# Batch 0's front in another order: zero products, V's spread and the release of the weights

## The chip, the cores and the metric

One core of one Trainium2 chip runs the kernel. The metric is the device time of one execution in microseconds (us); the time before is the median of three runs. Engines: PE (TensorE) multiplies, DVE (VectorE), ACT (ScalarE) and POOL (GpSimd) do the elementwise work, SP (SyncE) issues transfers. PE writes only into PSUM, and DVE or ACT copies from there.

## The reference

Eight batches of linear attention (8 heads, 576 positions, 64 features a head) and behind it a mixer with low rank along the positions and a two-layer network along the channels:

```python
def phi(x, c, s):                      # c, s: cos and sin of pi/2 * position / 576
    r = np.maximum(x, 0.0)
    return np.concatenate([r * c, r * s], axis=-1)
q_p, k_p = phi(q, cos_w, sin_w), phi(k, cos_w, sin_w)
kv  = np.einsum('bhsf,bhsd->bhfd', k_p, v)
num = np.einsum('bhsf,bhfd->bhsd', q_p, kv)
den = np.einsum('bhsf,bhf->bhs', q_p, k_p.sum(axis=2))[..., None] + 1e-06
x   = (num / den).transpose(0, 2, 1, 3).reshape(8, 576, 512)
u   = x + (x.transpose(0, 2, 1) @ U @ V).transpose(0, 2, 1)     # U 576x32, V 32x576
out = u + np.maximum(u @ w_ch1, 0.0) @ w_ch2                    # 512x2048, 2048x512
```

## The kernel before

**Tiling.** The 576 positions of a batch are four chunks of 128 (`c` = 0 to 3) and a tail of 64 (`c` = 4); the tails of two batches share one tile (`q_tl`, `k_tl`, `v_tl`, `x_tl`). q, k and v come in float32 into one staging tile each (`qst`, `kst`, `vst`), which every batch uses again; `load_odd` and `load_even` (L74, L68) fill a batch's odd and even partitions from SP's queue.

**Batch 0's front.** While q is on its way, PE multiplies zeros (`keep_warm`, L193). Then, chunk by chunk, `q_prep` makes the features (cos and sin, L258 on ACT, L260 on DVE; `FEATS` says which engine takes which), `qtr_mm` transposes them on PE (L328) and `qtr_evac` copies the transposes out. The same features for k follow, with `z_ps`, the sum of k's features over all positions (L807). `first_chain` then does all of batch 0 up to the mixer: casts of v (`v_block`, `v_prep`), `kv_unit` for heads 0 to 3 and 4 to 7 (L299), denominators (`den_mm`, L677; `recip`, L363 and L364), the products q times kv of half the heads for one chunk (`xh_mm`, L688) and their division (`xh_norm`, L697). `a_mm` (L715, L723) multiplies U by half the columns of x. `open_mm` (L730) puts the transposed x into PSUM, and `uTd_mm` (L488) adds the low-rank term to it, so that `uTd_evac` copies out u transposed, one of four blocks `d`. `spread_v` (L223, L226) brings V from 32 rows into the layout that `uTd_mm` and `u_unit` read (`V_bf`, `V_tl`).

**Mixer.** From `g1_main` (L523; hidden layer) and `g2_part` (L576; output) on, an order written out by hand puts the attention of the later batches beside the mixer's products: `at(j, ...)` for batch 1, `PLAN` for the rest. Batch 1's v is cast at slot 15, its kv products stand at slots 16 and 17.

**Queues and weights.** Each engine works in program order. POOL issues the loads of the weights, `w1_load` (L96) and `w2_load` (L102), four pieces each. Ahead of each group a copy of one element into `mark` makes POOL wait: in the kernel before for batch 0's v and for batch 1's v (heads 0 to 3).

**PSUM.** Tiles take buffers by tag: `X` one of two banks, `T` one bank, `o` two, `g` three (`O2`, `G3`, `T1` in the code). A new tile of a tag waits for the last reader of the one whose buffer it takes. `ORD`, the order of chunks behind kv, is (4, 0, 1, 2, 3).

Of the kernel before, what the change touches and what calls it, by code (L numbers as in the profile page):

```python
# [10 lines left out]
FP32 = mybir.dt.float32  # L11
# [6 lines left out]
def kernel(  # L18
# [15 lines left out]
    S = 576  # L34
    D = 64
    E = D + 1
    P = 128
# [5 lines left out]
    TS = 64  # L43
# [11 lines left out]
    ps = ctx.enter_context(tc.tile_pool(name="ps", bufs=1, space=bass.MemoryType.PSUM))  # L55
# [5 lines left out]
    kst = const.tile([P, H, 5, D], FP32)  # L61
# [44 lines left out]
    def cast(eng, o, i):  # L106
        if eng is nc.scalar:
            nc.scalar.activation(out=o, in_=i, func=AF.Copy, bias=0.0, scale=1.0)
        else:
            eng.tensor_copy(out=o, in_=i)  # L110
# [79 lines left out]
    def keep_warm(n, tag, bufs):  # L190
        w_ps = ps.tile([P, 512], FP32, tag=tag, bufs=bufs, name="w_ps")
        for _ in range(n):
            nc.tensor.matmul(out=w_ps, lhsT=zero[:, 0:P], rhs=zero, start=True, stop=True)  # L193
# [24 lines left out]
        for i in range(2):  # L218
            cast(G_, U_bf[tail(i), 4 + i, :], stU[tail(i), 4, :])

    def spread_v(eng):
        v_ps = ps.tile([P, 2, 512], FP32, tag="X", bufs=1, name="v_ps")
        nc.tensor.matmul(  # L223
            out=v_ps[:, 0, :], lhsT=four, rhs=V_nat[:, 0:512], start=True, stop=True
        )
        nc.tensor.matmul(  # L226
            out=v_ps[:, 1, 0:TS], lhsT=four, rhs=V_nat[:, 512:S], start=True, stop=True
        )
        cast(eng, V_bf, v_ps[:, 0, :].rearrange("r (c p) -> r c p", c=4))
        cast(eng, V_tl, v_ps[:, 1, 0:TS])  # L230


    k_p, q_p, q_pT, kv_sb, x_bf = {}, {}, {}, {}, {}
# [57 lines left out]
    def kv_unit(b, hg, tag, bufs, eng=None, n=E):  # L291
        if b not in kv_sb:
            kv_sb[b] = pool.tile([P, H, E], BF16, tag="kv", bufs=2, name="kv")
        acc = ps.tile([P, 4, n], FP32, tag=tag, bufs=bufs, name="kv_ps")
        vx = v_ext[b % 2]
        for i in range(4):
            h = hg * 4 + i
            for c in range(5):
                nc.tensor.matmul(  # L299
                    out=acc[:, i, :],  # L300
                    lhsT=k_of(b, c, h),
                    rhs=v_tl[:, h, 0:n] if c == 4 and b < 2 else vx[:, c, h, 0:n],
                    start=(c == 0),
                    stop=(c == 4),
                )
        cast(eng or V_, kv_sb[b][:, hg * 4 : hg * 4 + 4, 0:n], acc)
# [26 lines left out]
    def qtr_evac(b, c, eng, t):  # L333
        if c < 4:
            cast(eng, q_pT[b][:, c, :, :], t)
        else:
            cast(eng, q_tlT[:, :, tail(b)], t[:, :, 0:P:2])
# [24 lines left out]
    def recip(rec, den):  # L362
        nc.vector.tensor_scalar(out=rec, in0=den, scalar1=1e-6, scalar2=None, op0=ALU.add)  # L363
        nc.vector.reciprocal(out=rec, in_=rec)  # L364
# [42 lines left out]
    def A_of(b):  # L407
        return A_sb[b % 4]
# [57 lines left out]
    uT_ps = {}  # L466
# [16 lines left out]
    def uTd_evac(b, d, eng):  # L483
        cast(eng, uT[b][:, :, d, :], uT_ps[b, d])

    def uTd_mm(b, d):
        t = uT_ps[b, d]
        nc.tensor.matmul(  # L488
            out=t.rearrange("m c t -> m (c t)"), lhsT=A_of(b)[:, d * P : d * P + P],
            rhs=V_bf.rearrange("r c t -> r (c t)"), start=False, stop=True,  # L490
        )
# [182 lines left out]
    def den_mm(b, h0, h1, d_ps):  # L674
        for c in range(5):
            for h in range(h0, h1):
                nc.tensor.matmul(  # L677
                    out=d_ps[:, c, h - h0 : h - h0 + 1],
                    lhsT=qT_of(b, c, h),
                    rhs=z_sb[:, h : h + 1],  # L680
                    start=True,
                    stop=True,
                )

    def xh_mm(b, c, h0, tag, bufs):
        acc = ps.tile([P, 4, D], FP32, tag=tag, bufs=bufs, name="xh_ps")
        for h in range(h0, h0 + 4):
            nc.tensor.matmul(  # L688
                out=acc[:, h - h0, :], lhsT=qT_of(b, c, h), rhs=kv_sb[b][:, h, 0:D],
                start=True, stop=True,  # L690
            )
        return acc

    def xh_norm(b, c, h0, rec, acc):
        x_alloc(b)
        rows = slice(0, P) if c < 4 else tail(b)
        nc.vector.tensor_tensor(  # L697
            out=x_of(b, c, rows)[:, h0 * D : h0 * D + 4 * D].rearrange(
                "p (i d) -> p i d", d=D
            ),  # L700
            in0=acc[rows],
            in1=rec[rows, c, :].unsqueeze(2).to_broadcast([P if c < 4 else TS, 4, D]),
            op=ALU.mult,
        )
# [23 lines left out]
    def open_mm(b, d, t, cs):  # L728
        for c in cs:
            nc.tensor.matmul(  # L730
                out=t[:, c, :], lhsT=x_bf[b][:, c, d * P : d * P + P], rhs=ident,
                start=(c == 0), stop=False,
            )

    def first_chain(b):
        v_block(b, 0, 4, 0, 3, V_)
        v_block(b, 0, 4, 3, 4, A_)
        v_prep(b, 0, 4, (4,), (A_,))
        cast(V_, z_sb, z_ps)
        v_block(b, 4, 8, 0, 3, V_)  # L740
        v_block(b, 4, 8, 3, 4, A_)
        v_prep(b, 4, 8, (4,), (A_,))
        d0 = ps.tile([P, 2, 512], FP32, tag="X", bufs=1, name="d_ps")
        d = [d0[:, 0, 0:20].rearrange("p (c h) -> p c h", h=4)]
        rec = [pool.tile([P, 5, 4], FP32, tag="rec5", bufs=2, name="rec5") for _ in (0, 1)]
        kv_unit(b, 0, *T1, None, D)
        den_mm(b, 0, 4, d[0])
        recip(rec[0], d[0])
        x0 = [xh_mm(b, c, 0, *G3) for c in ORD[0:3]]
        for n in (0, 1):  # L750
            xh_norm(b, ORD[n], 0, rec[0], x0[n])
        kv_unit(b, 1, *O2, A_, D)
        x0.append(xh_mm(b, ORD[3], 0, *O2))
        d1 = ps.tile([P, 512], FP32, tag="T", bufs=1, name="d_ps")
        d.append(d1[:, 0:20].rearrange("p (c h) -> p c h", h=4))
        den_mm(b, 4, 8, d[1])
        x0.append(xh_mm(b, ORD[4], 0, *O2))
        for n in range(2, 5):
            xh_norm(b, ORD[n], 0, rec[0], x0[n])
            if n == 3:  # L760
                recip(rec[1], d[1])
        x1 = [xh_mm(b, c, 4, *t) for c, t in zip(ORD, (T1, G3))]
        spread_v(A_)
        x1 += [xh_mm(b, c, 4, *t) for c, t in zip(ORD[2:], (G3, G3, O2))]
        for n in range(5):
            xh_norm(b, ORD[n], 4, rec[1], x1[n])
        uT_alloc(b)
        u03 = ps.tile([P, 2, 512], FP32, tag="X", bufs=1, name="u03")
        t = [u03[:, i, :].rearrange("p (c t) -> p c t", c=4) for i in range(2)]
        a_ps = ps.tile([P, DM], FP32, tag="o", bufs=2, name="a_ps")  # L770
        a_mm(b, a_ps, 0, 256, range(5))
        cast(A_, A_of(b)[:, 0:256], a_ps[:, 0:256])
        for tag, bufs in (T1, O2):
            t.insert(-1, ps.tile([P, 4, P], FP32, tag=tag, bufs=bufs, name="uT_ps"))
        for i in range(4):
            uT_ps[b, i] = t[i]
        for i in range(2):
            open_mm(b, i, t[i], range(4))
        uTd_mm(b, 0)
        uTd_evac(b, 0, A_)  # L780
        uTd_mm(b, 1)
        uTd_evac(b, 1, V_)
        a_mm(b, a_ps, 256, 512, range(5))
        cast(A_, A_of(b)[:, 256:512], a_ps[:, 256:512])
        open_mm(b, 3, t[3], range(4))
        open_mm(b, 2, t[2], range(4))

    FEATS = [(V_, V_ if c == 3 else A_) for c in TL]
    qT_alloc(0)
    keep_warm(13, "X", 1)  # L790
    t_q = []
    for c in TL:
        tg = G3 if c < 3 else O2
# [1 line left out]
    for c in TL:  # L795
        q_prep(0, c, FEATS[c])
        qtr_mm(0, c, 0, H, t_q[c])
        keep_warm(1, "X", 1)
    for c, eng in zip(TL, (V_, A_, V_, A_, V_)):
        qtr_evac(0, c, eng, t_q[c])  # L800
    keep_warm(4, "X", 1)
    z_all = ps.tile([P, 2, 512], FP32, tag="X", bufs=1, name="z_ps")
    z_ps = z_all[:, 0, 0:H]
    for c in TL:
        k_prep(0, c, FEATS[c])
        for h in range(H):
            nc.tensor.matmul(  # L807
                out=z_ps[:, h : h + 1], lhsT=k_of(0, c, h), rhs=v_tl[:, 0, D:E],
                start=(c == 0 and h == 0), stop=(c == 4 and h == H - 1),
            )  # L810
        keep_warm(1, *G3)

    cast_uv()
    G_.tensor_copy(out=mark, in_=vst[0:TS, 3, 4, 0:1])
    for n in range(4):
        w1_load(n)
    first_chain(0)
    load_odd(qst, q, 1)
    load_even(qst, q, 1)
    load_odd(kst, k, 1)  # L820
# [1 line left out]
    for h0 in (0, 4):  # L822
        load_odd(vst, v, 1, h0, h0 + 4)
        load_even(vst, v, 1, h0, h0 + 4)
    G_.tensor_copy(out=mark, in_=vst[0:TS, 3, 4, 0:1])
    for n in range(4):
        w2_load(n)
    g1_main(0, 0, True)
# [109 lines left out]
```

## Time and profile before

| | |
|---|---|
| time, median of 3 (lowest, highest) | 313.95 us (313.73, 314.32) |
| the profiled execution: its time, its span | 311.89 us, 310.1 us |
| busy in the span: PE, DVE, ACT, POOL | 97%, 50%, 44%, 17% |
| granted TensorE clock | 1.0 |
| read from HBM, written | 36.86 MB, 9.44 MB |
| first product of the mixer (L523) | 22.46 us |

A line of a timeline gives start, duration, engine, line, operation, out<-in, shape and count, and in brackets the idle time before it and who ended it. A line of the chain gives start, duration, engine, tile, line. PE's products are pipelined and their ends modelled, so starts tell more than ends; the granted clock is given in tenths of full speed for 40 equal slices of the span.

### The profile page before, as it was taken

The page shows a single profiled execution, that of the slowest core. Times are in us where ns is not written, and L with a number is a line of the kernel's source. Part 1 is how long each engine was busy: PE and PEld are TensorE (multiplying, and loading weights), DVE is VectorE, ACT ScalarE, POOL GpSimd, SP SyncE. Part 2 cuts the span into 40 slices and gives each one's busy share as a digit, 9 for nine tenths or more (in the row PEclk, how much of TensorE's full clock was granted, in tenths as well). Part 3 has the DMA queues.
Part 4 walks back from the last instruction along what each step waited for, and adds up shares of the span by engine and source line. Part 5 has one row for each costly group of instructions (what it writes and reads, how often), then busy time and mean ns, then how long its engine had stood idle before and what let it go on. Part 6 is the DMA issues. An engine that isn't in the chain of part 4 may idle for free.

```text
span 310.1 us, 5750 instructions
## 1 busy us (share of the span) xinstructions
PE 301.9 (97%) x2341; PEld 157.7 (51%) x2341; DVE 155.0 (50%) x342; ACT 136.0 (44%) x229; POOL 52.9 (17%) x96
## 2 busy tenths in 40 slices
PE   5999999999999999999999999999999999999995
PEld 1676454446655444574455444574455444474443
DVE  4979834896878584146327583046426520002111
ACT  2936730264820466679300366669300366640000
POOL 8410400510131008004221300003321000000000
PEclk9999999999999999999999999999999999999999
DMA  7999999979997979982999879912981240001131
GB/s 216 354 258 255 197 187 274 326 143 241 288 191 142 314 133 251 243 242 82 180 212 322 207 127 234 273 47 53 194 154 60 75 80 0 0 2 68 70 101 68
DMA packets 86027, 53.21 MB, mean 172 GB/s; under 512 B 54258, under 2 KB 83218, under 8 KB 86002
## 3 DMA queue, kind: packets, MB, share of 16 engines
q1 hardware_dynamic: 79298, 41.36, 57.5%
q0 software_dynamic: 6560, 11.43, 15.0%
q8 instruction: 18, 0.29, 0.4%
q10 hardware_dynamic: 144, 0.07, 0.1%
q14 instruction: 7, 0.06, 0.0%
HBM read 36.86 MB, written 9.44 MB: 149 GB/s over the span
## 4 chain that ended last, share of the span: by engine, by line
PE 90%; DVE 5%; DMA 2%; issue 1%; ACT 0%; ACTq 0%; DVEq 0%
PE o_ps L576 40%; PE g_ps L523 32%; PE gt_ps L543 5%; PE kv_ps L299 3%; PE x_ps L390 3%; PE va_ps L435 2%; DMA qst<-in_q_dram 2%; DVE q_p L260 2%; DVE k_p L260 2%; PE a_ps L415 1%; PE t_ps L328 1%; PE t_ps L316 1%; PE w_ps L193 0%; PE va_ps L438 0%; PE xh_ps L688 0%
## 5 line engine op out<-in xcount | busy, mean ns | idle before, releaser
L532 ACT ACTIVATE hid<-g_ps 128x512 bf16<-128x512 f32 x128 | 76.2, 598 | 106.2 <-PE g_ps L523 106.2
L576 PE MATMUL o_ps<-w_bf,hid 128*128 128x512 bf16 (+2 forms) x528 | 120.0, 372 | 0.0
L523 PE MATMUL g_ps<-uT,w_bf 128*128 128x512 bf16 x512 | 117.6, 379 | 0.0
L523 PEld LDWEIGHTS <-w_bf 128*128 128x128 bf16 x512 | 48.9, 98 | 58.0 <-issue 2.1
L576 PEld LDWEIGHTS <-hid 128*128 128x128 bf16 x528 | 48.2, 98 | 50.8 <-issue 0.8
L586 DVE TENSOR_TENSOR o_sb<-u_bf,o_ps 128x512 f32<-128x512 bf16 (+2 forms) x33 | 22.1, 669 | 56.3 <-PE o_ps L576 56.2
L597 POOL DMA_DIRECT2D out_dram<-o_sb x24 | 15.2, 633 | 126.2 <-DVE o_sb L586 67.0
L442 DVE TENSOR_TENSOR u_bf<-x_bf,va_ps 128x512 bf16<-128x512 bf16 x32 | 21.8, 685 | 10.0 <-PE va_ps L435 9.9
L110 POOL CAST v_ext<-vst 128x512 bf16<-128x512 f32 (+1 forms) x28 | 20.1, 744 | 37.1 <-DMA vst<-in_v_dram 36.9
L110 DVE CAST kv<-kv_ps 128x260 bf16<-128x260 f32 (+1 forms) x15 | 6.4, 429 | 36.9 <-PE kv_ps L299 36.9
L400 DVE TENSOR_TENSOR x_bf<-x_ps,rec 128x512 bf16<-128x512 f32 x28 | 19.4, 691 | 1.0
L363 DVE TENSOR_SCALAR rec<-x_ps 128x8 f32<-128x8 f32 (+1 forms) x35 | 5.8, 165 | 22.8 <-PE x_ps L390 22.3
L543 PE MATMUL gt_ps<-uT_tl,w_bf 128*128 128x128 bf16 x256 | 15.9, 219 | 0.0
L260 DVE TENSOR_SCALAR q_p<-qst,cosw 128x512 bf16<-128x512 f32 x24 | 13.7, 583 | 2.9 <-DMA qst<-in_q_dram 2.9
L543 PEld LDWEIGHTS <-w_bf 128*128 128x128 bf16 x256 | 14.7, 98 | 0.9
L576 PE MATMUL o_ps<-w_bf,hid_tl 128*128 128x512 bf16 x64 | 14.8, 379 | 0.0
L390 PEld LDWEIGHTS <-q_pT 128*128 128x128 bf16 x224 | 10.7, 98 | 6.4 <-DVE x_bf L400 0.4
L258 ACT ACTIVATE k_p<-kst,sinw 128x512 bf16<-128x512 f32 x19 | 13.3, 712 | 0.0
L299 PEld LDWEIGHTS <-k_p 128*128 128x128 bf16 x256 | 11.1, 97 | 3.2 <-issue 0.3
L550 ACT ACTIVATE hid_tl<-gt_ps 128x512 bf16<-128x512 f32 x16 | 9.6, 597 | 6.6 <-PE gt_ps L543 6.6
L435 PE MATMUL va_ps<-A_sb,V_bf 128*128 128x512 bf16 x32 | 12.1, 379 | 0.1
L390 PE MATMUL x_ps<-kv,q_pT 128*128 128x65 bf16 x224 | 11.8, 194 | 0.0
(128 smaller groups left out, 233.0 us busy)
## 6 DMA issues: line engine op xcount, KB each, us to landing
qst<-in_q_dram SPq DMA_DIRECT2D x14, 512.0 KB, 6.3
kst<-in_k_dram SPq DMA_DIRECT2D x14, 512.0 KB, 8.6
vst<-in_v_dram SPq DMA_DIRECT2D x12, 512.0 KB, 8.1
out_dram<-o_sb POOLq DMA_DIRECT2D x24, 256.0 KB, 3.7
w_bf<-in_moe_w_ch_dram POOLq DMA_DIRECT2D x8, 512.0 KB, 11.1
out_dram<-o_sb SPq DMA_DIRECT2D x7, 256.0 KB, 2.4
qst<-in_q_dram SPq DMA_DIRECT2D x2, 640.0 KB, 6.4
kst<-in_k_dram SPq DMA_DIRECT2D x2, 640.0 KB, 10.8
```

The source lines that it names most:

```text
L110: eng.tensor_copy(out=o, in_=i)
L260: eng.tensor_scalar(out=o, in0=i, scalar1=0.0, scalar2=w, op0=ALU.max, op1=ALU.mult)
L299: nc.tensor.matmul(out=acc[:, i, :], lhsT=k_of(b, c, h), rhs=v_tl[:, h, 0:n] if c == 4 and b < 2 else vx[:, c, h, 0:n], start=(c == 0), st ...
L390: nc.tensor.matmul(out=acc[:, g, i * E : i * E + E], lhsT=qT_of(b, c, h), rhs=kv_sb[b][:, h, :], start=True, stop=True,)
L400: nc.vector.tensor_tensor(out=x_of(b, c, rows).rearrange("p (g i d) -> p g i d", g=2, d=D), in0=view[:, :, :, 0:D], in1=rec[rows].unsqueez ...
L435: nc.tensor.matmul(out=va, lhsT=V_bf[:, c, :], rhs=A_of(b), start=True, stop=True)
L442: nc.vector.tensor_tensor(out=u_bf[b][:, c, :] if c < 4 else u_tl[b // 2], in0=x_of(b, c), in1=va, op=ALU.add,)
L523: nc.tensor.matmul(out=g_ps.rearrange("p (c t) -> p c t", c=4), lhsT=w1_bf[:, d, j * P : j * P + P], rhs=uT[b][:, :, d, :], start=(d == 0) ...
L532: nc.scalar.activation(out=hid[b][:, j, :], in_=g_ps, func=AF.Relu, bias=0.0, scale=1.0)
L543: nc.tensor.matmul(out=g_ps[:, jj, :], lhsT=w1_bf[:, d, j * P : j * P + P], rhs=uT_tl[pr][:, d, :], start=(d == 0), stop=(d == 3),)
L576: nc.tensor.matmul(out=o[:, cols], lhsT=lhs[:, j, c * P : c * P + P], rhs=w2_bf[:, j, cols], start=(j == 0), stop=(j == NJ - 1),)
L586: nc.vector.tensor_tensor(out=o_sb[:, cols], in0=u[:, cols], in1=o[:, cols], op=ALU.add)
```

## The change

It has four parts. The zero products ahead of q go from 13 to 24, the single ones between q's transposes go, and the two features of one chunk on DVE are those of chunk 0 instead of chunk 3; chunk 0's transposes are copied out before chunk 2's features. V's spread moves from the middle of the second head group to the front: its products stand before `first_chain`, its copies on ACT behind the first `recip`. In `first_chain` the first kv goes out on ACT, the second kv product follows three `xh` products, all five divisions of the first head group come ahead of those of the second, `a_mm` and two `open_mm` come before the last second-group products, and copies change engines. The load of w_ch1 waits for batch 0's k, that of w_ch2 for batch 1's k.

```diff
--- before.py
+++ after.py
@@ -218,16 +218,19 @@
         for i in range(2):
             cast(G_, U_bf[tail(i), 4 + i, :], stU[tail(i), 4, :])
 
-    def spread_v(eng):
-        v_ps = ps.tile([P, 2, 512], FP32, tag="X", bufs=1, name="v_ps")
+    def spread_mm():
+        t = [ps.tile([P, 512], FP32, tag="o", bufs=2, name="v_ps") for _ in (0, 1)]
         nc.tensor.matmul(
-            out=v_ps[:, 0, :], lhsT=four, rhs=V_nat[:, 0:512], start=True, stop=True
+            out=t[0], lhsT=four, rhs=V_nat[:, 0:512], start=True, stop=True
         )
         nc.tensor.matmul(
-            out=v_ps[:, 1, 0:TS], lhsT=four, rhs=V_nat[:, 512:S], start=True, stop=True
-        )
-        cast(eng, V_bf, v_ps[:, 0, :].rearrange("r (c p) -> r c p", c=4))
-        cast(eng, V_tl, v_ps[:, 1, 0:TS])
+            out=t[1][:, 0:TS], lhsT=four, rhs=V_nat[:, 512:S], start=True, stop=True
+        )
+        return t
+
+    def spread_evac(eng, t):
+        cast(eng, V_bf, t[0].rearrange("r (c p) -> r c p", c=4))
+        cast(eng, V_tl, t[1][:, 0:TS])
 
 
     k_p, q_p, q_pT, kv_sb, x_bf = {}, {}, {}, {}, {}
@@ -732,7 +735,7 @@
                 start=(c == 0), stop=False,
             )
 
-    def first_chain(b):
+    def first_chain(b, v_ps):
         v_block(b, 0, 4, 0, 3, V_)
         v_block(b, 0, 4, 3, 4, A_)
         v_prep(b, 0, 4, (4,), (A_,))
@@ -740,54 +743,49 @@
         v_block(b, 4, 8, 0, 3, V_)
         v_block(b, 4, 8, 3, 4, A_)
         v_prep(b, 4, 8, (4,), (A_,))
-        d0 = ps.tile([P, 2, 512], FP32, tag="X", bufs=1, name="d_ps")
-        d = [d0[:, 0, 0:20].rearrange("p (c h) -> p c h", h=4)]
+        d_ps = ps.tile([P, 2, 512], FP32, tag="X", bufs=1, name="d_ps")
+        d = [d_ps[:, i, 0:20].rearrange("p (c h) -> p c h", h=4) for i in (0, 1)]
         rec = [pool.tile([P, 5, 4], FP32, tag="rec5", bufs=2, name="rec5") for _ in (0, 1)]
-        kv_unit(b, 0, *T1, None, D)
+        kv_unit(b, 0, *T1, A_, D)
         den_mm(b, 0, 4, d[0])
         recip(rec[0], d[0])
+        spread_evac(A_, v_ps)
         x0 = [xh_mm(b, c, 0, *G3) for c in ORD[0:3]]
-        for n in (0, 1):
+        kv_unit(b, 1, *T1, A_, D)
+        den_mm(b, 4, 8, d[1])
+        x0 += [xh_mm(b, c, 0, *O2) for c in ORD[3:5]]
+        for n in range(5):
             xh_norm(b, ORD[n], 0, rec[0], x0[n])
-        kv_unit(b, 1, *O2, A_, D)
-        x0.append(xh_mm(b, ORD[3], 0, *O2))
-        d1 = ps.tile([P, 512], FP32, tag="T", bufs=1, name="d_ps")
-        d.append(d1[:, 0:20].rearrange("p (c h) -> p c h", h=4))
-        den_mm(b, 4, 8, d[1])
-        x0.append(xh_mm(b, ORD[4], 0, *O2))
-        for n in range(2, 5):
-            xh_norm(b, ORD[n], 0, rec[0], x0[n])
-            if n == 3:
+            if n == 2:
                 recip(rec[1], d[1])
-        x1 = [xh_mm(b, c, 4, *t) for c, t in zip(ORD, (T1, G3))]
-        spread_v(A_)
-        x1 += [xh_mm(b, c, 4, *t) for c, t in zip(ORD[2:], (G3, G3, O2))]
-        for n in range(5):
-            xh_norm(b, ORD[n], 4, rec[1], x1[n])
+        x1 = [xh_mm(b, c, 4, *t) for c, t in zip(ORD, (T1, G3, G3, G3))]
+        xh_norm(b, ORD[0], 4, rec[1], x1[0])
         uT_alloc(b)
-        u03 = ps.tile([P, 2, 512], FP32, tag="X", bufs=1, name="u03")
-        t = [u03[:, i, :].rearrange("p (c t) -> p c t", c=4) for i in range(2)]
         a_ps = ps.tile([P, DM], FP32, tag="o", bufs=2, name="a_ps")
         a_mm(b, a_ps, 0, 256, range(5))
         cast(A_, A_of(b)[:, 0:256], a_ps[:, 0:256])
-        for tag, bufs in (T1, O2):
-            t.insert(-1, ps.tile([P, 4, P], FP32, tag=tag, bufs=bufs, name="uT_ps"))
-        for i in range(4):
-            uT_ps[b, i] = t[i]
+        u03 = ps.tile([P, 2, 512], FP32, tag="X", bufs=1, name="u03")
+        uT_ps[b, 0] = u03[:, 0, :].rearrange("p (c t) -> p c t", c=4)
+        uT_ps[b, 3] = u03[:, 1, :].rearrange("p (c t) -> p c t", c=4)
+        for i, (tag, bufs) in ((1, O2), (2, T1)):
+            uT_ps[b, i] = ps.tile([P, 4, P], FP32, tag=tag, bufs=bufs, name="uT_ps")
         for i in range(2):
-            open_mm(b, i, t[i], range(4))
-        uTd_mm(b, 0)
-        uTd_evac(b, 0, A_)
-        uTd_mm(b, 1)
-        uTd_evac(b, 1, V_)
+            open_mm(b, i, uT_ps[b, i], range(4))
+        xh_norm(b, ORD[1], 4, rec[1], x1[1])
+        x1.append(xh_mm(b, ORD[4], 4, *G3))
+        for n in range(2, 5):
+            xh_norm(b, ORD[n], 4, rec[1], x1[n])
+        for i in range(2):
+            uTd_mm(b, i)
+            uTd_evac(b, i, A_)
         a_mm(b, a_ps, 256, 512, range(5))
-        cast(A_, A_of(b)[:, 256:512], a_ps[:, 256:512])
-        open_mm(b, 3, t[3], range(4))
-        open_mm(b, 2, t[2], range(4))
-
-    FEATS = [(V_, V_ if c == 3 else A_) for c in TL]
+        cast(V_, A_of(b)[:, 256:512], a_ps[:, 256:512])
+        open_mm(b, 2, uT_ps[b, 2], range(4))
+        open_mm(b, 3, uT_ps[b, 3], range(4))
+
+    FEATS = [(V_, V_ if c == 0 else A_) for c in TL]
     qT_alloc(0)
-    keep_warm(13, "X", 1)
+    keep_warm(24, "X", 1)
     t_q = []
     for c in TL:
         tg = G3 if c < 3 else O2
@@ -795,10 +793,11 @@
     for c in TL:
         q_prep(0, c, FEATS[c])
         qtr_mm(0, c, 0, H, t_q[c])
-        keep_warm(1, "X", 1)
-    for c, eng in zip(TL, (V_, A_, V_, A_, V_)):
+        if c == 1:
+            qtr_evac(0, 0, V_, t_q[0])
+    for c, eng in ((1, A_), (2, V_), (3, V_), (4, A_)):
         qtr_evac(0, c, eng, t_q[c])
-    keep_warm(4, "X", 1)
+    keep_warm(6, "X", 1)
     z_all = ps.tile([P, 2, 512], FP32, tag="X", bufs=1, name="z_ps")
     z_ps = z_all[:, 0, 0:H]
     for c in TL:
@@ -808,13 +807,15 @@
                 out=z_ps[:, h : h + 1], lhsT=k_of(0, c, h), rhs=v_tl[:, 0, D:E],
                 start=(c == 0 and h == 0), stop=(c == 4 and h == H - 1),
             )
-        keep_warm(1, *G3)
+        if c < 4:
+            keep_warm(1, *G3)
 
     cast_uv()
-    G_.tensor_copy(out=mark, in_=vst[0:TS, 3, 4, 0:1])
+    G_.tensor_copy(out=mark, in_=kst[0:TS, 7, 4, 0:1])
     for n in range(4):
         w1_load(n)
-    first_chain(0)
+    v_ps = spread_mm()
+    first_chain(0, v_ps)
     load_odd(qst, q, 1)
     load_even(qst, q, 1)
     load_odd(kst, k, 1)
@@ -822,7 +823,7 @@
     for h0 in (0, 4):
         load_odd(vst, v, 1, h0, h0 + 4)
         load_even(vst, v, 1, h0, h0 + 4)
-    G_.tensor_copy(out=mark, in_=vst[0:TS, 3, 4, 0:1])
+    G_.tensor_copy(out=mark, in_=kst[0:TS, 7, 4, 0:1])
     for n in range(4):
         w2_load(n)
     g1_main(0, 0, True)
```

## Prediction

> **What bounds the kernel now.** I read the page first, then the chain that ended last between 14 and 24 us, then the timelines of PE, DVE and POOL there, then the landings of the transfers.
>
> ```profile
> PE 301.9 (97%) x2341; PEld 157.7 (51%) x2341; DVE 155.0 (50%) x342; ACT 136.0 (44%) x229; POOL 52.9 (17%) x96
> ...
> PEclk9999999999999999999999999999999999999999
> ```
>
> From the first product of the mixer on (22.46 us) PE issues without a gap over 0.5 us, so a change at the front is worth what it moves that point by, as long as weights and batch 1 arrive as much earlier. The chain ahead of it:
>
> ```profile
> 17.71 0.99 DVE x_bf L697 x3
> 18.71 0.10 DVE rec L363
> ...
> 18.85 0.41 PE xh_ps L688 x8
> 19.26 0.32 PE v_ps L223
> ...
> 19.60 0.59 PE xh_ps L688 x12
> 20.19 0.22 PE a_ps L715 x4
> ```
>
> DVE carries it to 18.8, then PE. Look at what PE has queued ahead of `a_mm` (L715), and when the data of `a_mm` is there (timeline of DVE, then of PE):
>
> ```profile
> 18.63 0.16 DVE L363 TENSOR_SCALAR rec<-d_ps 128x20 f32<-128x20 f32 x1
> 18.83 0.28 DVE L364 RECIPROCAL rec<-rec 128x20 f32<-128x20 f32 x1
> 19.02 0.36 DVE L697 TENSOR_TENSOR x_bf<-xh_ps,rec 128x256 bf16<-128x256 f32 x1
> 19.30 0.40 DVE L697 TENSOR_TENSOR x_tl<-xh_ps,rec 64x256 bf16<-64x256 f32 x1
> 19.63 1.43 DVE L697 TENSOR_TENSOR x_bf<-xh_ps,rec 128x256 bf16<-128x256 f32 x4
> ```
> ```profile
> 20.12 0.29 PE L715 MATMUL a_ps<-x_bf,U_bf 128*32 128x256 bf16 x4
> ...
> 21.47 0.29 PE L715 MATMUL a_ps<-x_bf,U_bf 128*32 128x256 bf16 x4
> ...
> 22.01 0.38 PE L730 MATMUL u<-ident,x_bf 128*128 128x128 bf16 x4 [0.22 <-ACT uT L108]
> ...
> 22.46 0.59 PE L523 MATMUL g_ps<-uT,w_bf 128*128 128x512 bf16 x2
> ```
>
> The first half of `a_mm` reads only heads 0 to 3, whose last normalisation ends at 19.02 + 0.36 = 19.38; it starts 0.74 us later because the second half's `xh` products and V's spread stand before it on PE. Last, the front and the releases of the weights:
>
> ```profile
> 1.19 3.03 PE L193 MATMUL w_ps<-zero 128*128 128x512 bf16 x7 [1.19 <-DVE zero L119]
> ...
> 8.15 0.62 PE L328 MATMUL t_ps<-ident,q_p 128*128 128x128 bf16 x8 [2.64 <-ACT q_p L258]
> ```
> ```profile
> 12.61 0.38 POOL L814 COPY mark<-vst 64x1 f32<-64x1 f32 x1 [3.40 <-DMA vst<-in_v_dram]
> 12.93 3.45 POOL L96 DMA_DIRECT2D w_bf<-in_moe_w_ch_dram  x4
> 33.46 0.18 POOL L825 COPY mark<-vst 64x1 f32<-64x1 f32 x1 [17.08 <-DMA vst<-in_v_dram]
> ```
>
> **Zero products, 13 to 24.** The first seven start 0.423 us apart ((3.03 - 0.49) / 6, the seventh being 0.49 long), later ones 0.216 (28 mixer products take 6.21: (6.21 - 0.38) / 27). The thirteen end at 5.51, so eleven more end at 5.51 + 2.38 = 7.89. q's first chunk now takes two DVE features: 7.40 + 0.40 + 0.48, and the transposes start at 8.37 (8.15 before). Cost 0; gain 0, since the eight transposes after the 2.64 us of idling already run at 0.056 us apiece ((0.62 - 0.22) / 7) and the granted clock is 9 throughout.
>
> **q's stage.** DVE: chunk 0 twice and chunk 1 once (0.40 each) to 8.6; the copy of chunk 0 now stands before chunk 2 and waits for its transposes, 8.37 + 0.62, so 9.02; copy 0.60, three features 1.23, two copies 1.20: k starts at 12.05, against 12.07. The idle time that DVE had (0.33 before the tail's copy) is spent earlier. ACT: four sines (0.61) to 9.85, one copy (0.95), then the tail's copy waits for the last transposes, 11.66, and takes 0.5: k's sines start at 12.2, not 11.72. They end at 14.74 and the first two v casts of ACT at 15.36 (14.89 before). PE needs the second of them 0.11 after the start of the kv products (15.43), so it just hides. The five single zero products dropped between transposes and the two added after them lie in PE's waits: 0.
>
> **V's spread early.** PE gets 0.22 + 0.06 for it between the z and kv products and loses one zero product (0.22): +0.06, but the last z product comes at 14.85 instead of 15.02. The kv products start at 15.3 to 15.45; I take -0.05. ACT's two copies (0.60, 0.22) go into its idle 2.38 us ahead of `kv`, 16.6 to 17.3, before the second kv product ends (17.8): 0. If they were late, the products that reuse their banks (x0's last two, 18.2) would be.
>
> **Chain of batch 0.** The first kv copy on ACT takes 0.39 instead of DVE's 0.43, but `recip` waits for the den products, which end at 16.66: 0. DVE: three normalisations from 17.30 (0.33 apart) to 18.30, `recip` 0.39 to the next start, two more: heads 0 to 3 are done at 19.40, as before. PE by then has issued all it may (four second-half products by 18.9), so `a_mm` starts at 19.46: -0.66. From there 0.82 to `uTd_mm` (20.94 - 20.12): 20.28. Its two copies, both on ACT (0.60, 0.49 apart), end at 21.33 and 21.83. DVE's remaining five normalisations end at 21.07, as now (19.63 + 1.43), so the second `a_mm` starts at 21.12: -0.35. Behind it 0.24, two groups of four transposes 0.22 each, without the 0.22 wait because the order is 2, 3: first mixer product at 21.81, -0.65. The copy of A's second half on DVE (0.43) ends at 21.91, before `uTd_mm` 2 at 22.25. The last normalisation, not PE's queue, is late next.
>
> **Transfers.** Batch 0's k lands 7.8 after 3.06, so w_ch1 is issued at 11.3. Its first piece took 9.0 (12.93 to 21.9); it is needed at 21.75. It shares engines with batch 1's q for longer: the rate is 356 GB/s for q, k, v alone (13 to 16 us) and 252 with both (19 to 33). Bounds 20.3 (9.0 again) and 21.9 (nothing won, +0.15); estimate 21.3: 0. w_ch2's first piece lands at 33.91 + 5.9 = 39.8, and PE takes it at 39.84: without an earlier release the 0.65 would be lost there. Batch 1's k lands at 15.11 + 13.8 = 28.9; a microsecond of sharing more, and w_ch2 is issued near 30, which covers it. The price is with batch 1's v: it lands at 20.02 + 15.9 = 35.9 and is read at 37.44, with casts of 1.76 before a product at 40.71. After the shift it may land as late as 38.3. With w_ch2 sharing its last part (the 252 rate instead of 356, two thirds of it lost to the weights) I estimate 36.4 to 38.2: 0; bounds 0 and +0.9. Batch 1's q (lands at 17.5, at the latest near 20.5 after) is read at 23.3.
>
> **Sum.** -0.65 - 0.05 = -0.70 (from -0.35, if the kv products come 0.1 later and a landing or a copy costs 0.2, to -1.05, if the second `a_mm` is also past its 0.35 of wait). Against the profiled execution: 311.89 (its span 310.1 and 1.8 around it) becomes 311.2. The median is 313.95, 2.06 above that execution; I carry the difference over: 313.25, own range 312.9 to 313.6. About 0.2% (0.63 us) is what a measurement of this kernel can tell from no change.
>
> **Rivals.** (1) *The zero products overrun q; slower.* With n products at 0.423, PE is free at 1.19 + 0.423 n + 0.216 (24 - n) = 6.37 + 0.207 n. It meets 8.37 at n = 9.7; each further one delays the transposes, DVE's copy of chunk 0 that now blocks the features behind it, and all the rest, by 0.207. Seven were slow here, thirteen could not overrun (6.7 at worst). The gain is gone from n = 13.1; n = 18 gives +1.73 - 0.70, 315.0. For it: the page has one execution. Against: the low spread of the runs shown (0.59 us). [...]
>
> (2) *Batch 1's v comes late.* It lands at 39.2 instead of by 38.3: +0.9, 314.2. For it: 17.6 to 22.2 SP's issues of v already take over 2 us each; against: DMA was idle to two thirds (share 0.35) from 34 to 36 us, and that time is what w_ch2 moves into.
>
> (3) *The zero products are worth more.* The 2.06 us between profiled and other executions could be a longer wait for q with the clock lost behind it, which eleven more products bridge: up to 2.06 more, 312.2 in the middle. Against: nothing in the trace shows a lost clock.
>
> **Chances.** Forecast 0.56 (0.37 faster, 0.19 the same); rival 1 0.15 (0.04 the same, 0.11 slower); rival 2 0.12 (0.06, 0.06); rival 3 0.13, faster; anything else 0.04, slower. Faster 0.50, the same 0.29, slower 0.21. 312.0 leaves out half of rival 3, 314.9 about half of rival 1 and the rest.
>
> **To look for.** Transposes of q at about 8.4 with no zero product in the way; k's features at 12.05; `a_mm` at 19.5 and 21.1, the first mixer product at 21.8; w_ch1's issue at 11.3, w_ch2's near 30; v_tl's cast of batch 1 without a DMA wait that reaches PE. A mixer that starts at 22.4 or a PE wait at 40 would make this wrong.

## The result and the profile after

The changed kernel takes 315.75 us (median of 21 runs, 313.64 to 317.35); the kernel before, in 21 runs beside it, 313.78 (311.93 to 316.4). The ratio is 1.006, with a 95% interval of 1.0038 to 1.0081: slower, outside the range 312.0 to 314.9, where 313.25 was forecast. The profiled execution took 315.9, with a span of 314.0. From its page (total, engine busy times, granted clock in 40 slices, the queue that carries instructions):

```profile
span 314.0 us, 5740 instructions
...
PE 306.1 (97%) x2322; PEld 161.4 (51%) x2348; DVE 154.1 (49%) x341; ACT 136.1 (43%) x230; POOL 51.7 (16%) x96
...
PEclk9957999999999999999999999999999999999999
...
q8 instruction: 18, 0.29, 0.4%
```

The PEclk line, all 9 before, shows a 5 and a 7 in the third and fourth slice (15.7 to 31.4 us). The trace's clock records place it: half speed from 16.45 to 26.69. That is 10.24 us, three times 3.41, the length of the stretches at half clock in e1 and e2 below. The windows view of the changed kernel shows the same stretch (window; length and PE busy; weight loads, DVE, ACT and POOL busy; then clock, DMA share, GB/s):

```profile
12.00:16.00 4.00, 3.25 (x45) 1.87 (x44) 4.00 (x9) 3.74 (x8) 2.42 (x4) 1.00 1.13 320
16.00:20.00 4.00, 4.00 (x79) 3.55 (x79) 2.19 (x8) 1.52 (x5) 0.00 (x0) 0.56 1.15 261
20.00:23.00 3.00, 3.00 (x63) 2.55 (x61) 2.30 (x9) 0.55 (x2) 0.00 (x0) 0.50 1.17 245
23.00:27.00 4.00, 3.78 (x33) 2.30 (x32) 1.24 (x4) 1.31 (x3) 0.00 (x0) 0.54 1.16 253
```

PE's timeline of the changed kernel (start, duration, then the operation; in brackets idle time and its releaser), with the events that the prediction had named:

```profile
1.19 7.82 PE L193 MATMUL w_ps<-zero 128*128 128x512 bf16 x24 [1.19 <-DVE zero L119]
8.84 1.06 PE L331 MATMUL t_ps<-ident,q_p 128*128 128x128 bf16 x16
...
13.98 0.35 PE L806 MATMUL z_ps<-v_tl,k_p 128*128 128x1 bf16 x8 [0.46 <-DVE k_p L263]
...
16.33 0.52 PE L223 MATMUL v_ps<-V_nat,four 32*128 32x512 bf16 x1
...
16.84 0.39 PE L302 MATMUL kv_ps<-v_ext,k_p 128*128 128x64 bf16 x4
...
22.33 0.40 PE L718 MATMUL a_ps<-x_bf,U_bf 128*32 128x256 bf16 x4
...
24.75 0.40 PE L718 MATMUL a_ps<-x_bf,U_bf 128*32 128x256 bf16 x4
...
25.96 0.96 PE L526 MATMUL g_ps<-uT,w_bf 128*128 128x512 bf16 x2
```

Against the kernel before, the kv products start 1.41 us later (16.84 against 15.43). From there to the first product of the mixer it takes 9.12 instead of 7.03 (22.46 - 15.43). The line of the kernel before:

```profile
15.43 0.28 PE L299 MATMUL kv_ps<-v_ext,k_p 128*128 128x64 bf16 x4
```

Behind the mixer's first product the two traces need almost the same: 314.0 - 25.96 = 288.04 and 310.1 - 22.46 = 287.64. So all but 0.4 of the 3.9 us between the spans arises ahead of 26 us. DVE's features of k and POOL's releases of the weights in the changed kernel:

```profile
12.57 0.60 DVE L263 TENSOR_SCALAR k_p<-kst,cosw 128x512 bf16<-128x512 f32 x1
13.10 0.82 DVE L263 TENSOR_SCALAR k_p<-kst,sinw 128x512 bf16<-128x512 f32 x1
...
15.37 0.47 DVE L263 TENSOR_SCALAR k_tl<-kst,cosw 128x512 bf16<-128x512 f32 x1
```
```profile
11.22 0.19 POOL L814 COPY mark<-kst 64x1 f32<-64x1 f32 x1 [1.49 <-DMA kst<-in_k_dram]
11.36 3.06 POOL L96 DMA_DIRECT2D w_bf<-in_moe_w_ch_dram  x4
31.05 0.23 POOL L826 COPY mark<-kst 64x1 f32<-64x1 f32 x1 [16.63 <-DMA kst<-in_k_dram]
```

The releases come where they were forecast. k's features start 0.50 later than before, and the six together take 3.27 (12.57 to 15.84) instead of 2.79.

Each run's mean granted clock is recorded, and the runs fall into two groups by it. Of the 100 runs of the kernel before that stand beside the experiments, 48 have 0.998 or more, with medians of 312.32, 312.08 and 312.11 in the three groups; 52 lie lower, mostly at 0.994 or 0.995, with 313.96, 313.90 and 313.85. Half the clock for one such stretch of 3.41 us is 0.5 x 3.41 / 314 = 0.5% of the mean, which is 0.995. Below, a run "keeps the clock" (or has the "full clock") if its mean is 0.998 or more. Of the 21 runs of the changed kernel one kept the clock (313.64), ten have 0.995, and ten lie between 0.983 and 0.993.

### The profile page after: what moved, and what is told of

The parts are those of the page before. It is cut to its first block, busy times and chain, and to the rows that moved or that the text cites. A ratio compares the mean times of both kernels' runs of the same rounds, so it can differ in the third digit from the quotient of the medians.

```text
span 314.0 us, 5740 instructions
## 1 busy us (share of the span) xinstructions
PE 306.1 (97%) x2322; PEld 161.4 (51%) x2348; DVE 154.1 (49%) x341; ACT 136.1 (43%) x230; POOL 51.7 (16%) x96
## 4 chain that ended last, share of the span: by engine, by line
PE 93%; DVE 4%; issue 1%; ACT 0%
PE o_ps L579 39%; PE g_ps L526 32%; PE gt_ps L546 5%; PE kv_ps L302 3%; PE x_ps L393 3%; PE w_ps L193 3%; PE va_ps L438 2%; DVE q_p L263 2%; DVE k_p L263 1%; PE a_ps L418 1%; PE xh_ps L691 1%; PE t_ps L319 1%; PE t_ps L331 1%; ACT k_p L261 0%; PE uT_ps L491 0%
## 5 line engine op out<-in xcount | busy, mean ns | idle before, releaser
L579 PE MATMUL o_ps<-w_bf,hid 128*128 128x512 bf16 (+2 forms) x509 | 118.0, 372 | 1.0
L110 POOL CAST v_ext<-vst 128x512 bf16<-128x512 f32 (+1 forms) x28 | 19.3, 716 | 38.0 <-DMA vst<-in_v_dram 34.8
L110 DVE CAST kv<-kv_ps 128x260 bf16<-128x260 f32 x14 | 6.0, 429 | 37.6 <-PE kv_ps L302 37.6
L302 PEld LDWEIGHTS <-k_p 128*128 128x128 bf16 x256 | 11.9, 101 | 3.5 <-issue 0.4
L302 PE MATMUL kv_ps<-v_ext,k_p 128*128 128x65 bf16 (+1 forms) x256 | 12.7, 199 | 0.0
L193 PE MATMUL w_ps<-zero 128*128 128x512 bf16 x33 | 10.7, 467 | 1.2 <-DVE zero L119 1.2
```

What stands on the lines that cost most here:

```text
L302: nc.tensor.matmul(out=acc[:, i, :], lhsT=k_of(b, c, h), rhs=v_tl[:, h, 0:n] if c == 4 and b < 2 else vx[:, c, h, 0:n], start=(c == 0), st ...
L579: nc.tensor.matmul(out=o[:, cols], lhsT=lhs[:, j, c * P : c * P + P], rhs=w2_bf[:, j, cols], start=(j == 0), stop=(j == NJ - 1),)
```

## Experiments

Four theories; the fourth was put up after the first four runs (e1 to e4). **Theory 1**: the clock is lost because the five single zero products between q's transposes and the one behind the last z product are gone. **Theory 2**: 24 zero products overrun q (rival 1). **Theory 3**: the earlier release of w_ch1 runs beside k's features on DVE and lengthens them, and z and kv come late. **Theory 4**: PE runs out of instructions. PE's instructions arrive in packets of 16 KB on queue q8 (0.29 MB in 18 packets on the page above), and in every trace that has a stop PE stops at about its 450th instruction, whatever that instruction is, until 2.2 to 2.7 us after such a packet has started. That q8 serves PE is read from counts: the page has 4670 products and weight loads on PE and 18 packets, about 259 to a packet, and of all the traces here the nine with up to 4790 records of PE have 18 packets, the five with 4804 or more have 19. The times of q8's packets and the count of PE's instructions (weight loads, products, semaphore operations) are taken from the trace itself.

**e1: the single zero products back (theory 1).**

```diff
         qtr_mm(0, c, 0, H, t_q[c])
+        keep_warm(1, "X", 1)
...
-        if c < 4:
-            keep_warm(1, *G3)
+        keep_warm(1, *G3)
```

> The changed kernel with the six single zero products put back (five behind q's transposes, one behind the last z product); 24 at the front stay. Theory 1 (lost clock: in the changed kernel's trace the granted clock is at half from 16.4 to 26.7 us, because PE has too little to do while q's and k's features are made): the clock is kept in most runs, mean granted clock 0.995 or more, the first mixer product comes near 23.5 instead of 25.96 us, and the median falls from 315.75 to about 313.6. Theory 2 (24 zero products run past q's arrival) and theory 3 (w_ch1's issue beside k's features slows DVE, 3.20 us for six features against 2.72): no change, 315.5 to 316.

315.79 (8 runs), ratio to before 1.0083 [1.0051, 1.0115]: no better than the changed kernel. PE's timeline and two windows of this run:

```profile
19.35 0.31 PE L691 MATMUL xh_ps<-kv,q_pT 128*128 128x64 bf16 x5
21.46 0.26 PE L691 MATMUL xh_ps<-kv,q_pT 128*128 128x64 bf16 x3 [1.80 <-issue]
```
```profile
16.00:20.00 4.00, 3.66 (x105) 3.03 (x103) 2.54 (x10) 2.01 (x7) 0.05 (x1) 1.00 1.18 256
20.00:23.00 3.00, 1.54 (x31) 1.20 (x31) 1.54 (x6) 0.27 (x1) 0.00 (x0) 0.84 1.17 245
```

Here z kept the clock, but in the middle of eight products that read the same data PE stands still for 1.80 us, released by "issue", that is by nothing the profile knows. Directly behind it, from 22.02 to 25.43, the clock is at half. Theory 1 falls as the account of the whole loss: the single products are back and the time is not. The stop is new.

**e2: 13 zero products instead of 24 (theory 2).** `keep_warm(24, "X", 1)` becomes `keep_warm(13, "X", 1)`.

> The changed kernel with 13 instead of 24 zero products ahead of q. Theory 2 (overrun): q's transposes start 0.3 to 0.8 us earlier and the median falls by 0.3 to 0.5 us, to about 315.3. Theory 1 (lost clock): the clock is lost as often or more, 315.8 or above, with longer stretches at half clock. Theory 3: no change.

316.04 (12 runs, one of them a stray at 1109.39 us), 1.0083 [1.0055, 1.0112]. That is theory 1's figure (315.8 or above), not theory 2's. Without the eleven products q's transposes start no earlier than 8.56, and PE idles ahead of them; this execution lost the clock from 8.78 to 12.19. The stop is there too, and behind it the clock is lost again (22.43 to 25.85):

```profile
8.56 1.72 PE L331 MATMUL t_ps<-ident,q_p 128*128 128x128 bf16 x16 [2.34 <-DVE q_p L263]
...
22.20 0.22 PE L691 MATMUL xh_ps<-kv,q_pT 128*128 128x64 bf16 x2 [1.61 <-issue]
```

The overrun of theory 2 is in the changed kernel's trace (8.84 against 8.56 here: 0.28), but taking it away gains nothing.

**e3: both weights released by v again (theory 3).**

```diff
-    G_.tensor_copy(out=mark, in_=kst[0:TS, 7, 4, 0:1])
+    G_.tensor_copy(out=mark, in_=vst[0:TS, 3, 4, 0:1])
```

> The changed kernel with both weight loads released by v again, as before the change. Theory 3 (the earlier issue slows DVE's k features): these six features take 2.7 us again instead of 3.2, the median falls by about 0.5 us, to 315.2, unless w_ch2's first piece then holds PE up near 43 us. Theories 1 and 2: 315.6 to 315.9, the clock lost as often as in the changed kernel (20 of its 21 runs show less than 1.0).

315.43 (11 runs), 1.0074 [1.0047, 1.0101]; not to be told from the changed kernel. k's features take 2.81 (12.61 to 15.42), and the kv products start at 16.18, so that part of theory 3 holds in this trace. The profiled execution kept the clock throughout (mean 1.0), and so shows the stop alone:

```profile
16.18 0.29 PE L302 MATMUL kv_ps<-v_ext,k_p 128*128 128x64 bf16 x4
...
19.13 0.26 PE L691 MATMUL xh_ps<-kv,q_tlT 128*128 128x64 bf16 x3
21.68 0.19 PE L691 MATMUL xh_ps<-kv,q_tlT 128*128 128x64 bf16 x1 [2.29 <-issue]
...
24.39 0.59 PE L526 MATMUL g_ps<-uT,w_bf 128*128 128x512 bf16 x2
```

From the first kv product to the mixer: 24.39 - 16.18 = 8.21 at full clock.

**e4: the kernel before with the new chain and V's spread early, and nothing else.**

> The kernel before with the new first_chain and V's spread early, and nothing else of the change: 13 zero products and the single ones, q's and k's features and the releases as before. Theory 1: the new order of the chain brings the 0.65 us that were forecast, 313.1 against 313.8 before, the first mixer product near 21.9 us where the clock is held. If the order itself costs time (a rival: copies on ACT and the spread on PE's way), 314.3 or more.

313.63 (12 runs), 1.0015 [0.9986, 1.0044]; its four runs with the full clock at 312.15.

```profile
17.59 0.29 PE L302 MATMUL kv_ps<-v_ext,k_p 128*128 128x64 bf16 x4
...
20.67 0.35 PE L691 MATMUL xh_ps<-kv,q_pT 128*128 128x64 bf16 x6
21.25 0.35 PE L691 MATMUL xh_ps<-kv,q_pT 128*128 128x64 bf16 x6 [0.23 <-issue]
...
23.96 0.59 PE L526 MATMUL g_ps<-uT,w_bf 128*128 128x512 bf16 x2
```

The kv products start at 17.59 in this execution, which lost the clock in the wait for q (0.57 on average from 8 to 12 us). To the mixer it is 23.96 - 17.59 = 6.37, 0.66 less than the 7.03 before, and since forms without any stop need 6.37 too (f1, g2, g3 below), the short stop (0.23) costs nothing here. In the trace the chain does what was forecast; 0.65 was the figure. The time shows less of it: 313.1 was expected, 313.63 came, and at full clock it is 312.15 against 312.32 for the kernel before in the same group, 0.17. Where the rest goes is open.

None of theories 1 to 3 explains a stop in the middle of a queue of ready products; theory 4 does. In the four, and in the kernel before and the changed one, the packet starts between 17.53 and 19.79, and PE goes on between 19.72 and 22.20, at the 449th of its records (the 450th in the kernel before). If so, more instructions ahead of that point must bring the packet earlier, whatever they compute.

**f1: the changed kernel with its 24 zero products of 512 columns cut into 96 of 128.** The work is the same; PE gets 144 instructions more (a weight load and a product each; the page of the kernel before counts 2341 of both).

```diff
+    def warm_128(n, tag, bufs):       # as keep_warm, with rhs=zero[:, 0:P] into w_ps[:, 0:P]
...
-    keep_warm(24, "X", 1)
+    warm_128(96, "X", 1)
```

> The changed kernel with its 24 zero products of 512 columns cut into 96 of 128: the same PE time, 144 more PE instructions (each product is a weight load and a matmul). Theory 4 (instruction fetch): in the changed kernel and its variants PE stops near its 450th instruction, in the second group's xh products, and goes on 2.2 to 2.4 us after a 16 KB packet of the instruction queue has started; with 144 instructions more the same point is reached before the kv products, and the packet is asked for before the weights' transfers fill the queues, so the stop of 0.2 to 2.3 us goes; 315.75 falls to 313.8 to 314.5. Theory 1 (the clock alone): no change, 315.5 to 316.

312.42 (12 runs), 0.9986 [0.9955, 1.0017] to the kernel before. The median is over 3 us below that of the changed kernel, which ran in another group; by the ratios to the kernel before, 1.006 and 0.9986, it is 0.7% (2.3 us), and the intervals do not overlap. The median is also below the 313.8 to 314.5 that theory 4 had expected, since without the stop most runs keep the clock too: eleven of the twelve (median of these 312.31), against one of 21 of the changed kernel. A line of its page, and PE's timeline:

```profile
q8 instruction: 19, 0.31, 0.4%
```
```profile
15.91 0.29 PE L309 MATMUL kv_ps<-v_ext,k_p 128*128 128x64 bf16 x4
...
18.99 0.54 PE L698 MATMUL xh_ps<-kv,q_pT 128*128 128x64 bf16 x12
19.62 0.60 PE L725 MATMUL a_ps<-x_bf,U_bf 128*32 128x256 bf16 x4
...
22.28 0.59 PE L533 MATMUL g_ps<-uT,w_bf 128*128 128x512 bf16 x2
```

One packet more has been moved, the first now starts at 10.95, and there is no stop: 15.91 to 22.28 is 6.37 again. The packet is earlier, not in a quieter moment: the mean share of the DMA engines is 1.11 from 9 to 11 us here, and 1.16 in the 2 us ahead of the changed kernel's packet.

**f2, f4: e4 with its 13 zero products replaced by 52, or by 72, of 128 columns.** `keep_warm(13, "X", 1)` becomes `warm_128(52, "X", 1)` (78 instructions more, the same columns) or `warm_128(72, "X", 1)` (118 more, 38% more columns).

> The kernel before with the new chain and the early spread of V only, and its 13 zero products cut into 52 of 128 columns (78 more PE instructions). Theory 4: the stop of 0.43 us that the uncut version shows at PE's 450th instruction goes; median 313.2 instead of 313.63, the runs with full clock near 311.6 instead of 312.15; kv products to first mixer product 5.9 to 6.0 us. Theory 1: no change from 313.63.

> As f2 with 72 zero products of 128 columns, worth 18 of 512, so that PE's wait for q falls from 2.4 to about 1.4 us. Theory 1 (the clock is lost where PE does too little in one window of 3.41 us; in the kernel before this happens in the wait for q in about half of the runs): most runs keep the full clock, median 312.0 to 312.5, below the kernel before by 1 us. If the wait for q is not what loses the clock: as f2, 313.2.

f2 takes 313.82, 1.0021 [0.9991, 1.0050], f4 312.35, 0.998 [0.9955, 1.0005]; 4 and 12 of 12 runs keep the clock. f2 missed its expectation: the first packet starts at 18.71 and the stop is still there. But it has wandered, from the second half's `xh` products back into the kv products, 78 instructions earlier in the program, and again it is at the 450th instruction. In f4 the packet starts at 13.49, nothing stops PE, and the last wait before the mixer is for w_ch1, which is still released by v there. f2, then f4:

```profile
21.21 0.19 PE L309 MATMUL kv_ps<-v_tl,k_tl 128*128 128x64 bf16 x1 [0.95 <-issue]
```
```profile
23.04 0.61 PE L533 MATMUL g_ps<-uT,w_bf 128*128 128x512 bf16 x2 [0.37 <-DMA w_bf<-in_moe_w_ch_dram]
```

**e5: the kernel before with 24 zero products.** `keep_warm(13, "X", 1)` becomes `keep_warm(24, "X", 1)`.

> The kernel before with 24 instead of 13 zero products of 512 columns and nothing else. Theory 1 and 2: fewer runs lose the clock in the wait for q, some start q's transposes up to 0.9 us late; median 312.9 to 313.3 against 313.4. Theory 4: 22 PE instructions more move the 450th into the first xh products of the chain; if the fetch is not there by then, PE stops there by 0.5 to 2 us and the median is 313.8 or above.

314.18 (12 runs), 1.0021 [0.9988, 1.0054]; 5 of 12 keep the clock, about as often as the kernel before. The median is what theory 4 had said, the stop (0.36) is shorter. More zero products of the old size do not hold the clock by themselves. The stop has moved ahead in the program again (into the first `xh` products), and w_ch1 is late:

```profile
19.50 0.25 PE L688 MATMUL xh_ps<-kv,q_tlT 128*128 128x64 bf16 x3 [0.36 <-issue]
...
24.31 0.39 PE L523 MATMUL g_ps<-uT,w_bf 128*128 128x512 bf16 x1 [1.17 <-DMA w_bf<-in_moe_w_ch_dram]
```

**g2, g3: two more forms of the changed kernel.** g2 has `warm_128(72, "X", 1)` for its 24 (96 instructions more, a quarter fewer columns). g3 keeps the 24 of 512 columns and adds 32 products of one column behind the transposes of q's second chunk (64 instructions more, hardly any work):

```diff
         if c == 1:
+            warm_1(32, "X", 1)        # rhs=zero[:, 0:1] into w_ps[:, 0:1]
             qtr_evac(0, 0, V_, t_q[0])
```

> The changed kernel with 72 instead of 24 zero products, of 128 columns (18 of 512 in time; 96 PE instructions more than the changed kernel, 48 fewer than f1). Theory 2 (24 overrun q's arrival when the clock is freed late): q's transposes never wait for zeros, 0.1 to 0.4 us less than f1 (312.42), 312.1. Theory 4: no stop at the 450th instruction, as in f1.

> The changed kernel with its 24 zero products of 512 columns as they are, and 32 products of one column (64 PE instructions, 0.8 us of issue) behind the transposes of q's chunk 1, where PE waits 0.8 us anyway. It tells the number of instructions from the shape of the products at the front. Theory 4: the instruction packet starts 3 us or more earlier than 19.33, the stop at the 450th instruction is gone or under 0.3 us, kv products to first mixer product 6.4 to 6.6 us in a run with full clock, median 313 to 313.8. If the 128-column products helped f1 by holding the clock in another way: as the changed kernel, 315.5 to 316.

g2: 312.40, 0.9986 [0.9956, 1.0016], 11 of 12 with the full clock; the 0.1 to 0.4 below f1 that theory 2 had expected are not there. g3: 312.88, 1.0006 [0.9977, 1.0035], 9 of 12. The packet starts at 13.86 and 14.79, and neither has a stop. g3 is the control for the shape of the zero products: they are as in the changed kernel, and still almost 3 us of the median are gone (by the ratios 0.5%, 1.7 us; the intervals just miss each other).

```profile
15.94 0.29 PE L309 MATMUL kv_ps<-v_ext,k_p 128*128 128x64 bf16 x4
...
19.02 0.54 PE L698 MATMUL xh_ps<-kv,q_pT 128*128 128x64 bf16 x12
19.65 0.60 PE L725 MATMUL a_ps<-x_bf,U_bf 128*32 128x256 bf16 x4
...
22.31 0.59 PE L533 MATMUL g_ps<-uT,w_bf 128*128 128x512 bf16 x2
```

These lines are g3's: 15.94 to 22.31 is 6.37 for the third time; g2 has 16.57 to 22.94.

**g1, g4: the releases once more, without the stop.** g1 is f4 with both releases by k, g4 is f1 with both by v.

> The kernel before with the new chain, the early spread of V, both weight loads released by k, and 72 zero products of 128 columns. In f4 (the same with the releases by v) PE waited 0.37 us at the first mixer product for w_ch1's first piece, which landed at 22.99. Theory 4 with the forecast's view of the transfers: the piece lands by 21.5, the first mixer product comes near 22.0 to 22.4, median 311.9 against 312.35 for f4. If the earlier release costs more than it gives (k's features on DVE beside POOL's issues): 312.4 or more.

> f1 (the changed kernel with 96 zero products of 128 columns) with both weight loads released by v again. The forecast's view: DVE makes k's six features in 2.7 instead of 3.1 us, but w_ch1's first piece lands after 22.3 and the first mixer product waits for it; median 312.6 to 313.2 against 312.42. If the releases do not matter: 312.2 to 312.5.

g4: 314.1, 1.0027 [0.9995, 1.0059]; its nine runs with the full clock lie at 313.66, against 312.31 for f1, which ran in another group. This pair favours the release by k, but the intervals overlap, and g4's profiled execution (mixer at 22.80) does not show where the 1.3 us go. g1: 313.4, 1.0007 [0.9974, 1.0039], a miss, and against f4 (312.35) the pair points the other way. What the releases are worth without the stop is not shown. Six of g1's twelve runs keep the clock, at 312.2; the profiled one lost it from 15.84 to 22.67:

```profile
16.00:20.00 4.00, 4.00 (x70) 3.09 (x68) 1.72 (x7) 1.71 (x5) 0.00 (x0) 0.50 1.18 247
```

No stop precedes this; it comes at the end of the z products, as in the changed kernel's profile. g1 differs from f4, which keeps the clock in all twelve runs, in the releases alone; why g1 loses it in half its runs, and g2, with the same release, in one of twelve, is open.

## Why the prediction was wrong

**The step that failed** is in the chain of batch 0: "PE by then has issued all it may", so that `a_mm` was to start at 19.46; in the changed kernel's trace it starts at 22.33. The chain was worked out as if PE could take at once whatever was ready, and the clock was carried over as "9 throughout". In the traces with a stop PE stands at its 449th or 450th record until 2.2 to 2.7 us after a packet of 16 KB has started on q8. The zero products were priced "Cost 0; gain 0" and the dropped single ones "0", since they lie in waits; but each is two instructions, and the stop moves in the program with their number (f2's 78 more put it 78 instructions earlier). With 64, 96 and 144 more (g3, g2, f1) the packet starts at 14.79, 13.86 and 10.95 instead of 19.33, and the stop is gone. In the kernel before PE's records show a gap of 0.14 us ahead of the 450th; in the chain's new order the stop is 0.23 to 2.29 us long in the five executions that have the full clock just ahead of it (e1 to e4, f2). At full clock it makes the chain 8.21 instead of 6.37 (e3), 1.84 more.

The later packets cost nothing that shows. Counted on from the 449th record in steps of 259, the page's mean to a packet (the 708th, the 967th and so on), each of them has started at least 9.0 us before PE reaches that record in the changed kernel's trace. PE does not stop there: from the first stop's end to 313 us the one gap of over 0.12 us in its records is 0.22 at 24.18. The first packet is another matter: PE waited up to 2.29 us for it (e3).

**The lost clock** is the second part. e1 and e2 show a stop of 1.6 to 1.8 us and the clock halved right behind it; without the stop f1, g2 and g3 keep it in 31 of 36 runs, with it the changed kernel in one of 21 and e1 to e3 in four of 30 (e2's stray run left out). The profiled execution of the changed kernel is another case: it lost the clock at the end of the z products (16.45), and the stop that came 5 us later left only 0.25 between two weight loads (21.30 to 21.55), so nearly all of its loss is half clock. That most of the 20 lose it behind the stop, as e1 and e2 do, is inferred from g3, whose z products follow in the same order and which keeps the clock in 9 of 12; it is not shown run by run, and g1 loses the clock in half its runs with no stop in its trace. Why it was lost at 16.45 is open. The stretches at half clock last 3.41 us in e1 and e2, 6.83 in g1 and 10.24 in the changed kernel: once, twice and three times 3.41. That the clock is lost where PE does too little in 3.41 us, as f4's expectation has it, was the author's theory and is not shown: a stop of 2.29 us left the clock as it was (e3).

**Sizes.** Five runs with the stop and the full clock (one of the changed kernel, two each of e1 and e3) have group medians of 313.64, 315.15 and 314.64, against 312.31 for f1: 1.3 to 2.8 for the stop, an estimate, since the three come from two other groups of runs than f1. The rest, up to the median of 315.75, goes with the lost clock.

**Point by point.**
- *Chain, -0.65*: right where nothing stops PE: 6.37 instead of 7.03 in e4, f1, g2 and g3, -0.66. In the changed kernel itself it is 9.12.
- *kv products, -0.05*: wrong even without the stop. They start at 15.94 in g3's trace, +0.51: k's features start 0.27 later (q came 0.23 later in that execution), take 0.05 more, and V's spread ahead of the kv products costs the other 0.19, where 0.06 less a z product 0.17 earlier was set. In the changed kernel's trace the term is +1.41: 0.50 for k's start, 0.48 for its longer features, the rest the spread at half clock and the z products. With +0.51 for -0.05 the sum of -0.70 becomes -0.15, and g3's mixer starts at 22.31 instead of 22.46.
- *Zero products*: rival 1's mechanism was there. Twelve were slow instead of seven (the clock records turn to full speed at 6.21 us instead of 3.95), the 24 ended at 9.01, and the transposes started at 8.84, not 8.37; the rival's formula gives 8.85 for twelve. (The terms written down for 8.37 add up to 8.28; f1, g2 and g3 show 0.97 to 0.98 from DVE's first feature to the transposes, which gives 8.37 or 8.38.) Its price is 0.28 by e2, one execution of each: not what made the kernel slower.
- *q's stage, k at 12.05*: 12.57, for that overrun and a q that landed 0.16 later.
- *Transfers, 0*: right. w_ch1 was issued at 11.36 and landed at 19.75; w_ch2 was issued at 31.50, with its first piece landing at 38.37, ahead of its reader at 43.67. Batch 1's v landed at 35.9. Rival 2 did not occur. Not foreseen: POOL's issues beside k's features.
- *Rival 3*: its premise, a lost clock, was right; it got 0.13 because the one profiled execution shows none. Its remedy was not: 24 zero products by themselves do not hold the clock (e5). Most of the 2.06 us carried from the profile to the median is a lost clock in half of the runs (313.9 against 312.1), not a constant. When the stop is gone, the changed kernel keeps the clock in most runs (31 of 36), and that, not the chain, is what its median gains.

At equal clock the best forms are no faster than the kernel before: f1 312.31, g2 312.32 and f4 312.35, against 312.08 to 312.11 in the same groups. Their medians are 0.3 to 1.2 below its median because it loses the clock in half its runs; no interval excludes 1.

**Open.** When PE asks for the packet. The 194th instruction, about one packet's 259 ahead of the 450th, comes at 8.08 to 11.66 in the traces without a stop and at 13.11 to 16.21 in those with one, so the added instructions bring this point forward. But the packet starts 2.5 to 5.6 us after it, and 1.2 to 3.8 after the 222nd, so neither count is the trigger alone. The DMA traffic and the clock in the wait for q differ between the traces and were not varied by themselves.

## What to carry to other kernels

When PE idles with "issue" as releaser in the middle of products that read the same data, count its instructions and look for the instruction queue's packet: here the stop stayed at the 449th or 450th record whatever stood there, and filler that put 64 to 144 instructions more ahead of it (g3, g2, f4, f1) brought the packet in before it was needed, while 22 and 78 more (e5, f2) did not. Price a product that only keeps PE busy as instructions as well as time. And before the difference between one profiled execution and the median is carried as a constant, look whether the runs fall into groups by their granted clock.

## What was not expected of the hardware

- The stop for the first 16 KB packet lasts 0.14 to 2.29 us, and PE goes on 2.2 to 2.7 us after the packet has started (the packet itself takes 0.9 to 1.1 us). The later packets, each at least 9.0 us ahead, stop nothing in the changed kernel's trace.
- A stop of 1.6 us was followed by half the clock for 3.41 us (e2); one of 2.29 us was not (e3).
- POOL's four issues of w_ch1 beside DVE's six features of k came in two forms: 3.05 or 3.06 us with features of 3.27 to 3.46 (the changed kernel, g1, g2), or 3.61 with 2.84 (f1, g3).
